# Token mixing with one level of Strassen: seven block products in place of eight, in two passes over the contraction tokens

## The chip, the cores and the metric

The kernel runs on one core of a Trainium2 chip. The metric is the device time of one execution in microseconds (us). Where there are several executions, the median is given with the lowest and highest. In the profile PE is TensorE (matrix multiplication), PEld its weight load, DVE is VectorE, ACT is ScalarE, POOL is GpSimd and SP is SyncE, which here only issues transfers; a "q" after an engine's name marks the engine's queue. "L384" is line 384 of the kernel that was profiled, so line numbers differ between variants.

## The reference

A long convolution per channel gives `y` (8 batches, 5696 tokens, 128 channels). Then comes the block that this study is about:

```python
theta = y @ w_theta                      # 128 x 128
zr, zi = y * cos(theta), y * sin(theta)  # "phases"
yr = einsum('ts,bsd->btd', w_tok_r, zr)  # token mixing: two 5696 x 5696 matrices
yi = einsum('ts,bsd->btd', w_tok_i, zi)
u = y + yr + yi
out = u + maximum(u @ w_ch, 0)           # w_ch 128 x 128
```

Token mixing is one product `[w_tok_r w_tok_i] x [zr; zi]`: 5696 output tokens, 2 x 5696 contraction tokens, 8 x 128 = 1024 columns. It is by far the largest part of the work.

## The kernel before

The kernel works in stages: convolution; phases of all 45 token tiles (128 tokens each), whose zr and zi go to memory; a load of all z tiles into SBUF; then token mixing, one output tile after the other. The core of the last stage, with cuts:

```python
z_sb = zp.tile([P, NK, BD], BF16)                 # all of zr and zi, NK = 89 contraction tiles
for c in range(NBC): ...                          # a few large loads on SyncE's queue

def load(ti, c, ng):                              # weights: 32-partition loads on GpSimd's queue
    wb = wp.tile([P, 4, BJ * 64 + REM], BF16, tag="wb")
    for i in range(4):
        nc.gpsimd.dma_start(wb[32 * i:32 * i + 32, :ng, :w], ...)
    return wb
# weights(): VectorE transposes 32 x 32 blocks of wb into wt            [cut]
# tail(): adds y, transposes, multiplies by w_ch, stores                [cut]
pend = []
for ti in range(NT):
    ps = [kps.tile([P, 512], F32, tag=f"ps{h}") for h in range(2)]   # pool kps has bufs=2
    for c in range(NBC):
        wb = load(ti, c, m // 32)
        for j0 in range(0, BJ, CJ):
            for k, wt in weights(wb, c, j0, min(CJ, BJ - j0), m // 32):
                for h in range(2):
                    nc.tensor.matmul(ps[h][:m], wt, z_sb[:, k, h * 512:(h + 1) * 512],
                                     start=(k == 0), stop=(k == NK - 1))
            if c < 2 and j0 == CJ and pend:
                tail(*pend.pop(0))                # the tile before is finished here
    pend += [(ti, m, ps[0], 0), (ti, m, ps[1], 1)]
```

Both accumulators are double-buffered, so that the next tile starts while the last one is evicted. And the finishing work of a tile stands in the middle of the next tile, where its inputs are long there.

## Time and profile before

The time is 2781.31 us, median of 2 runs (2780.08 to 2782.54).

The page of the profiled run gives busy times and, in 40 equal slices of the span, the busy tenths of each engine. "PEclk" is the granted clock of TensorE in tenths, "DMA" the busy tenths of the 16 transfer engines.

```profile
PE 2399.3 (86%) x15345; PEld 1314.6 (47%) x15345; DVE 1038.9 (37%) x1401; ACT 483.6 (17%) x401; POOL 494.1 (18%) x775
...
PE   4788888886332259999999999999999999999998
...
DVE  5544444445999012322232222322232223222231
...
PEclk7699999998555579999999999999999999999999
DMA  9977777776523985555555555555555555555552
```

Read across: the convolution fills the first nine slices. Then VectorE is at 9 while TensorE is at 3 (phases), then the transfers are at 9 and nearly nothing else works (the z loads), and from about slice 15 TensorE is full to the end.

The view by windows gives the same for stretches: start and end in us, length, busy time and instruction count of each engine, granted clock, transfer share and GB/s.

```profile
664.00:900.00 236.00, 83.92 (x720) 71.64 (x720) 229.37 (x225) 152.01 (x137) 102.66 (x45) 0.51 0.40 148
905.00:1035.00 130.00, 44.98 (x163) 17.92 (x164) 8.79 (x14) 0.00 (x0) 9.54 (x18) 0.63 0.99 211
1200.00:1600.00 400.00, 400.00 (x1979) 185.03 (x1978) 116.89 (x195) 12.59 (x20) 86.32 (x161) 1.00 0.56 95
```

| stage before | time | what limits it |
|---|---|---|
| convolution | to 664 us | not touched by the change |
| phases | 664 to 900 us | VectorE, 229 of 236 us busy: 5.2 us per tile |
| z loads | 900 to about 1028 us (the last lands at 1027.6) | transfers, share 0.99 at 211 GB/s |
| mixing | to the end | TensorE, 400 of 400 us busy at clock 1.00; 39.3 us per output tile |

In mixing a 512-column matrix product starts every 0.216 us (1300.00, 1300.22, 1300.43, ... in the timeline). The Trainium skill, "TensorE: Matmul & The Clock Gate", part 1, gives 215.7 ns for that size at full clock and 426.7 ns in the throttled state; the first agrees here. A full engine at full clock can only be relieved by fewer products.

### The profile page before, as it was taken

The page shows a single profiled execution, that of the slowest core. Times are in us where ns is not written, and L with a number is a line of the kernel's source. Part 1 is how long each engine was busy: PE and PEld are TensorE (multiplying, and loading weights), DVE is VectorE, ACT ScalarE, POOL GpSimd, SP SyncE. Part 2 cuts the span into 40 slices and gives each one's busy share as a digit, 9 for nine tenths or more (in the row PEclk, how much of TensorE's full clock was granted, in tenths as well). Part 3 has the DMA queues.
Part 4 walks back from the last instruction along what each step waited for, and adds up shares of the span by engine and source line. Part 5 has one row for each costly group of instructions (what it writes and reads, how often), then busy time and mean ns, then how long its engine had stood idle before and what let it go on. Part 6 is the DMA issues. An engine that isn't in the chain of part 4 may idle for free.

```text
span 2782.4 us, 36609 instructions
## 1 busy us (share of the span) xinstructions
PE 2399.3 (86%) x15345; PEld 1314.6 (47%) x15345; DVE 1038.9 (37%) x1401; ACT 483.6 (17%) x401; POOL 494.1 (18%) x775
## 2 busy tenths in 40 slices
PE   4788888886332259999999999999999999999998
PEld 1377777775332024444444444444444444444444
DVE  5544444445999012322232222322232223222231
ACT  3444344445665000000000000000000000000000
POOL 0000000001444002222222222222222222222220
PEclk7699999998555579999999999999999999999999
DMA  9977777776523985555555555555555555555552
GB/s 249 219 175 176 170 176 177 175 180 189 200 102 106 228 176 98 98 94 91 95 97 93 94 92 97 98 93 95 98 98 94 91 95 97 93 94 92 97 98 35
DMA packets 261108, 348.81 MB, mean 125 GB/s; under 512 B 27472, under 2 KB 221392, under 8 KB 260816
## 3 DMA queue, kind: packets, MB, share of 16 engines
q0 software_dynamic: 108384, 131.28, 30.8%
q1 hardware_dynamic: 152128, 213.56, 30.0%
q8 instruction: 121, 1.98, 0.3%
q10 hardware_dynamic: 432, 1.64, 0.2%
q14 instruction: 43, 0.35, 0.0%
HBM read 417.40 MB, written 60.23 MB: 172 GB/s over the span
## 4 chain that ended last, share of the span: by engine, by line
PE 72%; DMA 14%; DVE 9%; SPq 3%; issue 2%; ACT 0%; DVEq 0%; POOL 0%; ACTq 0%; POOLq 0%
PE psum L155 9%; DMA strip<-h_pad 9%; SPq L225 3%; DVE zr L194 2%; DVE mag L185 2%; DMA tmp<-in_x_dram 2%; DVE red L182 2%; DMA z_sb<-zi_hbm 2%; DVE yT L174 1%; DMA h_bf<-in_h_dram 1%; DVE strip L150 1%; DVE strip L144 1%; PE v L284 1%; PE utp L279 1%; PE ps_20849 L301 1%
## 5 line engine op out<-in xcount | busy, mean ns | idle before, releaser
L301 PEld LDWEIGHTS <-wt 128*128 128x128 bf16 (+1 forms) x7920 | 771.4, 98 | 997.1 <-issue 112.4
L255 DVE STREAM_TRANSPOSE wt<-wb 128x512 f32<-128x512 f32 (+1 forms) x540 | 357.0, 661 | 1219.8 <-PE ps_9186 L301 96.1
L155 PE MATMUL psum<-x_sb,strip 128*128 128x360 bf16 (+44 forms) x5760 | 483.2, 243 | 72.8 <-DVE strip L144 37.1
L155 PEld LDWEIGHTS <-strip 128*128 128x128 bf16 x5760 | 410.8, 98 | 146.0 <-DVE strip L144 42.9
L245 POOL DMA_DIRECT2D wb<-in_moe_w_tok_r_dram x360 | 194.6, 545 | 1445.2 <-DVE wt L255 1104.8
L276 ACT ACTIVATE ub<-u 128x512 bf16<-128x512 f32 (+1 forms) x90 | 56.7, 630 | 1821.4 <-DVE u L274 1821.4
L159 ACT ACTIVATE y_sb<-psum 128x360 bf16<-128x360 f32 x128 | 227.5, 1778 | 329.1 <-PE psum L155 329.1
L195 POOL TENSOR_TENSOR zi<-sin_sb,y_sb 128x1024 bf16<-128x1024 f32 x45 | 102.7, 2282 | 792.7 <-ACT sin_sb L189 784.5
L245 POOL DMA_DIRECT2D wb<-in_moe_w_tok_i_dram x360 | 194.6, 545 | 9.8 <-issue 9.5
L144 DVE COPY strip<-strip 64x2944 bf16<-64x2944 bf16 (+1 forms) x128 | 115.3, 904 | 164.2 <-DMA strip<-h_pad 150.2
L150 DVE COPY strip<-strip 64x2944 bf16<-64x2944 bf16 (+1 forms) x128 | 115.6, 906 | 159.6 <-DMA strip<-h_pad 131.3
L177 PE MATMUL theta_ps<-w_theta_sb,yT 128*128 128x128 bf16 x360 | 49.1, 308 | 144.1 <-DVE yT L174 144.0
L301 PE MATMUL ps_9185<-z_sb,wt 128*128 128x512 bf16 x88 | 39.2, 445 | 97.6 <-DMA z_sb<-zi_hbm 97.6
L177 PEld LDWEIGHTS <-yT 128*128 128x128 bf16 x360 | 35.2, 138 | 156.1 <-DVE yT L174 156.1
L113 PE MATMUL rps<-tmpbf,R_bf 128*128 128x512 bf16 x90 | 46.5, 620 | 50.5 <-DVE tmpbf L110 50.1
L194 DVE TENSOR_TENSOR zr<-cos_sb,y_sb 128x1024 bf16<-128x1024 f32 x45 | 84.2, 1874 | 4.3 <-ACT cos_sb L190 4.3
L286 DVE SCALAR_TENSOR_TENSOR u<-v,u 128x512 f32<-128x512 f32 (+1 forms) x90 | 62.2, 691 | 52.3 <-PE v L284 52.3
L185 DVE TENSOR_SCALAR mag<-red 128x1024 int32<-128x1024 int32 x45 | 69.6, 1580 | 0.0
L110 DVE CAST tmpbf<-tmp 128x1024 bf16<-128x1024 f32 x45 | 56.7, 1267 | 33.4 <-DMA tmp<-in_x_dram 33.2
L180 ACT ACTIVATE rnd<-theta_ps,magic 128x1024 f32<-128x1024 f32 x45 | 50.0, 1113 | 47.4 <-PE theta_ps L177 47.4
L115 ACT ACTIVATE x_sb<-rps 128x1024 bf16<-128x1024 f32 x45 | 46.1, 1024 | 58.2 <-PE rps L113 58.1
L190 ACT ACTIVATE cos_sb<-mag,half_pi 128x1024 f32<-128x1024 f32 x45 | 51.6, 1147 | 23.4 <-DVE mag L185 23.4
(306 smaller groups left out, 3504.0 us busy)
## 6 DMA issues: line engine op xcount, KB each, us to landing
strip<-h_pad SPq DMA_DIRECT2D x128, 376.0 KB, 4.4
wb<-in_moe_w_tok_r_dram POOLq DMA_DIRECT2D x264, 176.0 KB, 3.8
wb<-in_moe_w_tok_i_dram POOLq DMA_DIRECT2D x264, 176.0 KB, 4.9
strip<-h_pad SPq DMA_DIRECT2D x128, 360.0 KB, 5.1
tmp<-in_x_dram SPq DMA_DIRECT2D x44, 512.0 KB, 5.8
out_dram<-u SPq DMA_DIRECT2D x88, 256.0 KB, 2.3
wb<-in_moe_w_tok_r_dram POOLq DMA_DIRECT2D x88, 184.0 KB, 3.7
wb<-in_moe_w_tok_i_dram POOLq DMA_DIRECT2D x88, 184.0 KB, 5.7
```

Source lines behind the costliest of these rows:

```text
L144: nc.vector.tensor_copy(strip[64:, :w], strip[:64, 64:w + 64])
L150: nc.vector.tensor_copy(strip[:64, 64:w + 64], strip[64:, :w])
L155: nc.tensor.matmul(psum[:, B * k: B * k + B * ntj], strip[:, c:c + P], x_sb2[:, d, :B * ntj], start=(k == 0), stop=(k == NT - 1))
L159: nc.scalar.activation(y_sb[:, :, :, d].rearrange("q t b -> q (t b)"), psum, AF.Copy)
L177: nc.tensor.matmul(theta_ps[:, bb * D:(bb + 1) * D], yT[:, b, :], w_theta_sb, start=True, stop=True)
L185: nc.vector.tensor_scalar(mag.bitcast(mybir.dt.int32), red.bitcast(mybir.dt.int32), 0x7FFFFFFF, None, op0=ALU.bitwise_and)
L194: nc.vector.tensor_mul(zr, cos_sb, yflat)
L195: nc.gpsimd.tensor_mul(zi, sin_sb, yflat)
L225: nc.sync.dma_start(z_sb[32 * i:32 * i + 32, 2 * BJ * c:2 * BJ * (c + 1), :].rearrange("p (j r) n -> p j (r n)", r=2), bass.AP(tensor=zsrc ...
L245: nc.gpsimd.dma_start(wb[32 * i:32 * i + 32, :ng, :w], bass.AP(tensor=a.tensor, offset=a.offset + ti * P * S + (i % 2) * Q + c * BJ * 64, ...
L255: nc.vector.transpose(wt.rearrange("p j g t r -> p (j g t r)").bitcast(F32).rearrange("p (j g t) -> p g j t", j=CJ, g=4)[:, :ng, :nj], wb[ ...
L301: nc.tensor.matmul(ps[h][:m], wt, z_sb[:, k, h * 512:(h + 1) * 512], start=(k == 0), stop=(k == NK - 1))
```

## The change

Intent: split output tokens, contraction and columns in halves and form the 2 x 2 block product by Strassen's seven products M1 to M7 in place of eight. Two output tiles ("a pair": tile t and tile 22 + t) times 1024 columns are then made together, 7 accumulators of 128 x 512. The seven combinations of z are kept in SBUF for half of the tokens at a time (11 x 2 x 7 x 512 values of 2 bytes, 158 KB in each of 128 partitions), so the contraction is done in two passes of 22 tiles; pass 1 leaves partial results in memory and pass 2 adds them. Pass 1 needs the phases of only the first 22 tiles, and the other 23 are done as half tiles during pass 1. The 64 leftover tokens are done apart. The core of the diff, with cuts:

```diff
-    with tc.tile_pool(name="s2", bufs=3) as tsb, ...:         # phases of all 45 tiles
-        for ti in range(NT): ...
+        for ti in order:                                       # 22 tiles
+            phases(ti, y_sb[:, ti, :, :], 0, B, sb1, tps, thp)
...
+        def load_b(p):                                         # operand sums of one pass
+            for j in range(NJ):                                # NJ = 11
+                bt = bp.tile([P, 2, 7, 512], BF16, tag=f"b{j}")
+                tb = tbp.tile([P, 2, 2, 512], BF16, tag="tb")
+                for i in range(4):
+                    nc.sync.dma_start(bt[q, :, M2, :], z_rows(zr_hbm, r0, 2, 2, 0))
+                    nc.sync.dma_start(bt[q, :, M5, :], z_rows(zi_hbm, r0, 2, 2, 512))
+                    nc.sync.dma_start(tb[q, :, 0, :], z_rows(zr_hbm, r0, 2, 2, 512))
+                    nc.sync.dma_start(tb[q, :, 1, :], z_rows(zi_hbm, r0, 2, 2, 0))
+                nc.vector.tensor_sub(bt[:, :, M3, :], b12, b22)      # and four more
...
+        def finish(p, ti, h, c, m=P):
+            if p == 0:
+                nc.gpsimd.dma_start(c[:m], y2_hbm[ti]..., accum_op=add)   # c += y
+                nc.sync.dma_start(cp_hbm[ti]..., c[:m])                   # partial result
+                return
+            nc.gpsimd.dma_start(c[:m], cp_hbm[ti]..., accum_op=add)       # c += partial
+            # copy to bf16 (ACT), transpose (PE), copy (ACT), product with w_ch (PE), max and add, store
...
+        def pair(p, tt, bts, zl):
+            ms = [mps.tile([P, 512], F32, tag=f"m{q}") for q in range(7)]   # pool mps has bufs=1
+            for ci, (j0, nj) in enumerate(CHUNKS):                          # 3 chunks: 4, 4, 3 steps
+                a11 = w_t(moe_w_tok_r, top, p, j0, nj)   # 4 loads on GpSimd, 1 transpose on VectorE
+                a12 = w_t(moe_w_tok_i, top, p, j0, nj)
+                a22 = w_t(moe_w_tok_i, bot, p, j0, nj)
+                a21 = w_t(moe_w_tok_r, bot, p, j0, nj)
+                for q in (M5, M3, M4, M2, M1, M7, M6):
+                    if q == M5: a = w_sum(a11, a12, add, nj)                # VectorE
+                    elif q == M3: a = a11
+                    elif q == M4: a = a22
+                    elif q == M2: a = w_sum(a21, a22, add, nj)
+                    ...
+                    for j in range(nj):
+                        for r in range(2):
+                            nc.tensor.matmul(ms[q], a[:, j, :, r], bts[j0 + j][:, r, q, :], ...)
+                if p == 0:
+                    background(1 if ci < 2 else 0)       # a half tile of phases
+            nc.scalar.activation(c11, ms[M5], AF.Copy)
+            nc.vector.tensor_add(c12, ms[M3], c11)
+            nc.scalar.activation(c22, ms[M3], AF.Copy)
+            nc.vector.tensor_sub(c11, ms[M4], c11)
+            ...                                          # M2, M1, M7, M6 likewise
+            finish(p, tt, 1, c12); finish(p, 22 + tt, 0, c21)
+            finish(p, tt, 0, c11); finish(p, 22 + tt, 1, c22)
```

## The prediction

> **What bounds it now.** The stage windows show three parts: convolution to about 664 us; phases of 45 token tiles to 900 us (VectorE busy all the time, 5.2 us per tile); token mixing to the end. Mixing first waits for its z tiles (DMA busy share about 1.0 until about 1035 us). Then TensorE is 100% busy at granted clock 1.00: 1973 matmuls in 400 us, 39.3 us per output tile of 178 matmuls of 512 columns, so about 0.216 us each. That is the floor for this work; only fewer matmuls help. VectorE is 29% busy there, GpSimd (weight-load issues, 0.545 us each in the groups view) 22%.
>
> **What the change removes.** 8,010 wide matmuls become about 7,120: 22 pairs x 154 in each pass, plus leftovers. That is 890 x 0.216 = 190 us of TensorE. 23 of the 45 phase tiles leave the serial stage: 23 x 5.2 = 120 us. Loads before mixing halve: some 50 us. Gross gain 310 to 360 us.
>
> **What it adds, per pair (33.2 us of matmuls).**
> - VectorE: 12 transposes (0.71/0.58 us, 8 us), 15 bf16 sums (estimate 0.6 us for 1024 elements, two per cycle; the Trainium skill, "VectorE: DVE Perf Modes", "What auto-detection actually checks"; no run shows it yet), 8 PSUM additions at 0.65 us, and phases or final steps: about 26 us. Busy, not full.
> - GpSimd: 48 weight issues x 0.545 = 26 us, plus four accumulating loads: about 30 us.
> - Seven PSUM accumulators of one buffer each and one shared "misc" bank. Nothing is double-buffered across pairs, and VectorE, GpSimd and the DMA queue are in order.
>
> The instruction order shows what this costs. In a pair's last chunk VectorE evicts M3/M5 before it transposes a22 for M4, and evicts M4 before transposing a21 for M2: about 2 us of idle TensorE each. In pass 1 a half-tile of phases (transpose, copy, matmul, ACT, VectorE) sits in TensorE's order just there: 4 to 5 us more. At the pair's end GpSimd's accumulating loads wait for the last eviction, and the next pair's a22 and a21 loads stand behind them (landing 3.8 to 4.9 us in the DMA issues list). In pass 2 the final transposes and channel matmuls, which need the accumulated tile, stand in TensorE's order ahead of M4, through the single misc bank: another 7 us.
> I estimate 10 to 13 us of idle TensorE per pair, so 46 us in pass 1 and 48 in pass 2 (before: 2 x 39.3 = 78.7 per two output tiles; after: 94).
>
> **Sum.** Conv 664 + phases 115 + pair 0 with loading 80 + 21 x 46 + left rows 25 + pair 0 again 80 + 21 x 48 + end 35 = about 2970; I take 2940, as stalls may overlap. With only 6 us of stalls per pair it would be about 2740.
>
> Predicted 2940 us, 80% range 2760 to 3110. Faster by over 2%: 0.13; within 2%: 0.18; slower: 0.69.
>
> **What shows it.** Right: in steady pairs TensorE busy about 75 to 80%, its idle time ended by VectorE (transposes, sums) in the last chunk and first chunk; in pass 2 by ACT's copies for the final steps; pair period 44 to 50 us; a second load gap of 30 us or more between passes; granted clock dipping below 1. VectorE below 70%. The phase stage must end near 780 us.
> Wrong: pair period near 36 to 38 us with TensorE over 90% busy.
>
> **What would make it wrong.** Accumulating loads landing in 2 us and weight prefetch deep enough to hide the boundary (faster); sums at one element per cycle, slow 512-byte weight packets, or idle gaps halving TensorE's clock (slower).

## The result, and the profile after

The kernel takes 3258.15 us, median of 2 runs (3245.34 and 3270.97), and is correct. The ratio to the kernel before is 1.171, with a 95% interval of 1.152 to 1.191. It is 17% slower. The direction of the prediction was right, but the time lies 148 us above the upper end of its range.

The page of the changed kernel, the same lines as before:

```profile
PE 2415.1 (74%) x14377; PEld 1237.3 (38%) x14377; DVE 1612.0 (50%) x2462; ACT 623.1 (19%) x696; POOL 1536.0 (47%) x2598
...
PE   4788888942587777777777787578887787877777
...
DVE  5544444486465454544454545455554445454443
...
PEclk7899999955698888888888888789999999999898
DMA  9877777766576767676767667767768677776865
```

968 fewer PE instructions (the prediction had counted on 890) take 16 us more of PE time, because they no longer all run at full clock; and PE is never at 9 in mixing. No other engine is full either: this is a kernel of waits, not of work.

The windows: phases and the first loads (the last phase product ends at 772.9), the load ramp of pass 1, nine pairs of pass 1, and a stretch of pass 2.

```profile
664.00:780.00 116.00, 34.15 (x288) 29.14 (x288) 99.00 (x100) 66.08 (x62) 60.06 (x34) 0.50 0.53 186
798.00:870.00 72.00, 38.21 (x96) 12.23 (x97) 29.70 (x52) 0.00 (x0) 31.01 (x59) 0.67 0.62 118
1044.00:1528.00 484.00, 362.61 (x1526) 149.11 (x1526) 235.78 (x387) 51.31 (x81) 284.46 (x483) 0.87 0.68 108
2650.00:3150.00 500.00, 389.04 (x1863) 175.03 (x1862) 245.61 (x421) 61.76 (x105) 325.32 (x582) 0.93 0.73 97
```

A regular mark in the trace, ScalarE's last copy of an accumulator in each pair, gives the periods. They make the sum of the prediction measurable term by term:

| term | predicted | measured | excess |
|---|---|---|---|
| convolution and phases | 779 | 773 | -6 |
| first pair of pass 1, with loading | 80 | 133 | 53 |
| 21 pairs of pass 1 | 21 x 46 = 966 | 1097 (52.3 each; 53.5 in the steady part) | 131 |
| boundary: leftover rows, loading, first pair of pass 2 | 25 + 80 = 105 | 146 | 41 |
| 21 pairs of pass 2 | 21 x 48 = 1008 | 1045 (49.8 each; 51.5 in the steady part) | 37 |
| end | 35 | 49 | 14 |
| sum | 2973 | 3243 (span of the profiled run) | 270 |

Per steady pair of pass 1, the window gives 362.6 / 484 x 53.5 = 40.1 us of busy TensorE and 13.4 us idle. At 0.216 us the 154 products are 33.2 us, with the phases' small products about 34.2; so the half clock costs about 6 us. The idle time is what I had predicted (10 to 13 us); the clock was not in my sum. In pass 2 the idle time is 111.0 / 500 x 51.5 = 11.4 us, and the busy time again 40.1 us.

The waits of TensorE at the end of a pass-1 pair, from the timeline of PE (start, duration, operation, count; in brackets the idle time before and what ended it). In this view, every group of two products should last 0.59:

```profile
1520.94 0.61 PE L384 MATMUL m_12667<-b_8370,out__12940 128*128 128x512 bf16 x2 [0.73 <-DVE out__12940 L295]
...
1524.95 0.61 PE L384 MATMUL m_12666<-b_8370,wt 128*128 128x512 bf16 x2 [2.55 <-DVE wt L273]
...
1527.56 0.40 PE L174 MATMUL tpz<-ident_bf,yb 128*128 128x128 bf16 x4 [1.14 <-DMA yb<-y_hbm]
1528.47 0.40 PE L178 MATMUL theta_ps<-w_theta_sb,yT 128*128 128x128 bf16 x4 [0.52 <-DVE yT L175]
1531.97 1.03 PE L384 MATMUL m_12664<-b_8370,out__12960 128*128 128x512 bf16 x2 [3.10 <-DVE out__12960 L295]
1532.80 1.06 PE L384 MATMUL m_12664<-b_8393,out__12960 128*128 128x512 bf16 x2
...
1548.81 1.03 PE L384 MATMUL m_13018<-b_8186,wt 128*128 128x512 bf16 x2 [4.52 <-DVE wt L273]
```

After the waits the groups last 1.06 in place of 0.59, and start 0.85 us apart in place of 0.43: half clock (0.427 us per product, as the skill's page has it), until about 1537.9. The last wait, 4.52 us, belongs already to the next pair: its product M4, which needs a22 (loads from w_tok_i). VectorE's own timeline shows what stood before that transpose (the view names a load from w_tok_r; the a22 loads share their semaphores with others, and in the trace the last of them lands at 1547.96, just before the transpose), and GpSimd's queue shows why the weights came late (L303 is an accumulating load, L267 a weight load):

```profile
1548.05 0.71 DVE L273 STREAM_TRANSPOSE wt<-wb 128x512 f32<-128x512 f32 x1 [5.71 <-DMA wb<-in_moe_w_tok_r_dram]
```

```profile
1536.34 0.92 POOL L303 DMA_DIRECT2D c_12994<-y_hbm  x1 [4.88 <-DVE c_12994 L401]
1536.91 0.92 POOL L267 DMA_DIRECT2D wb<-in_moe_w_tok_i_dram  x1
1540.00 0.86 POOL L303 DMA_DIRECT2D c_12992<-y_hbm  x1 [2.17 <-DVE c_12992 L404]
1540.57 0.85 POOL L267 DMA_DIRECT2D wb<-in_moe_w_tok_i_dram  x1
1541.29 1.02 POOL L303 DMA_DIRECT2D c_12995<-y_hbm  x1
1541.86 1.57 POOL L267 DMA_DIRECT2D wb<-in_moe_w_tok_i_dram  x2
1542.95 2.65 POOL L267 DMA_DIRECT2D wb<-in_moe_w_tok_r_dram  x4
```

GpSimd issues in order. Its accumulating loads need the finished tile c, hence the last eviction, hence the end of the pair's last products; the next pair's four a22 loads stand between and behind them. The first is issued at 1536.91, the last two in the row that starts at 1541.86; the last lands at 1547.96, is transposed at 1548.05, and TensorE goes on at 1548.81. So the wait has two parts, the late issue and the landing, which took 5.6 us for the last load; over the whole run the median for loads of this size is 3.7 to 4.0 us. In pass 2 the wait before such a load is longer still, and the waits of TensorE are of three kinds (eviction ahead of a transpose, eviction ahead of a sum, finishing work that waits for ScalarE):

```profile
2687.05 0.92 POOL L307 DMA_DIRECT2D c_21112<-cp_hbm  x1 [11.57 <-DVE c_21112 L404]
```

```profile
2728.36 0.61 PE L384 MATMUL m_21204<-b_16567,wt 128*128 128x512 bf16 x2 [1.90 <-DVE wt L273]
...
2731.69 0.61 PE L384 MATMUL m_21202<-b_16567,out__21444 128*128 128x512 bf16 x2 [1.86 <-DVE out__21444 L295]
...
2745.19 0.40 PE L313 MATMUL utp<-ident_bf,ub 128*128 128x128 bf16 x4 [2.47 <-ACT ub L310]
```

ScalarE's copy in turn waited for the landing of the accumulating load, and so did the next one (TensorE waited 1.88 us for that):

```profile
2744.50 0.63 ACT L310 ACTIVATE ub<-c_21493 128x512 bf16<-128x512 f32 x1 [13.31 <-DMA c_21493<-cp_hbm]
...
2748.13 0.63 ACT L310 ACTIVATE ub<-c_21494 128x512 bf16<-128x512 f32 x1 [1.86 <-DMA c_21494<-cp_hbm]
```

In pass 2 these loads therefore hold TensorE through the finishing work; whether the weights behind them hold it there too is not shown.

The load ramp at the start of each pass, in SyncE's queue, VectorE beside it. Each of the 11 steps has 16 such issues, 0.64 us apart, on one queue:

```profile
805.26 0.59 SPq L251 DMA_DIRECT2D b_8232<-zi_hbm  x1
805.90 0.59 SPq L252 DMA_DIRECT2D tb<-zr_hbm  x1
806.53 0.59 SPq L253 DMA_DIRECT2D tb<-zi_hbm  x1
```

```profile
799.56 0.69 DVE L259 TENSOR_TENSOR b_8209<-b_8209 128x1024 bf16<-128x1024 bf16 x1 [6.16 <-DMA b_8209<-zi_hbm]
...
810.47 0.69 DVE L259 TENSOR_TENSOR b_8232<-b_8232 128x1024 bf16<-128x1024 bf16 x1 [7.73 <-DMA b_8232<-zi_hbm]
```

A step takes 10.7 us in the median (10.9 here, 799.56 to 810.47), and 16 x 0.64 = 10.2 us of it are the issues; some steps are longer, up to 13.4 us. SyncE's queue also waits until the sums have freed the single tile tb, about 10 us in the whole first ramp by the view of its waits. Meanwhile the transfers are not full: share 0.62, 118 GB/s, against 0.99 and 211 GB/s in the load stage of before.

So there are three theories for the 270 us of excess, not exclusive: the ramp is bound by issue on one queue (94 us in two terms); the pair is held by a chain through GpSimd's ordered queue (accumulating loads ahead of weight loads) and by the order of evictions on VectorE; or the half clock itself is the cost. Rivals: the engines or the transfers are at their limit with the new work.

### The profile page after: what moved, and what is told of

The parts are those of the page before. It is cut to its first block, busy times and chain, and to the rows that moved or that the text cites. A ratio compares the mean times of both kernels' runs of the same rounds, so it can differ in the third digit from the quotient of the medians.

```text
span 3243.6 us, 39671 instructions
## 1 busy us (share of the span) xinstructions
PE 2415.1 (74%) x14377; PEld 1237.3 (38%) x14377; DVE 1612.0 (50%) x2462; ACT 623.1 (19%) x696; POOL 1536.0 (47%) x2598
## 5 line engine op out<-in xcount | busy, mean ns | idle before, releaser
L267 POOL DMA_DIRECT2D wb<-in_moe_w_tok_r_dram x1080 | 636.4, 709 | 173.0 <-DVE wt L273 114.5
L267 POOL DMA_DIRECT2D wb<-in_moe_w_tok_i_dram x1080 | 638.9, 666 | 70.7 <-issue 17.6
L192 POOL TENSOR_TENSOR zi<-red,y_sb 128x1024 bf16<-128x1024 f32 x22 | 55.2, 2528 | 712.1 <-DMA y_hbm<-y_sb 663.5
L384 PEld LDWEIGHTS <-wt 128*128 128x128 bf16 x1936 | 197.7, 107 | 450.8 <-DVE wt L273 213.8
L181 ACT ACTIVATE red<-theta_ps,magic 128x512 f32<-128x512 f32 (+1 forms) x68 | 55.9, 823 | 865.8 <-PE theta_ps L178 853.4
L192 POOL TENSOR_TENSOR zi<-red,yb 128x512 bf16<-128x512 f32 x46 | 62.8, 1364 | 263.8 <-issue 219.3
L182 DVE SCALAR_TENSOR_TENSOR red<-red,theta_ps 128x512 f32<-128x512 f32 (+1 forms) x68 | 57.6, 857 | 154.3 <-ACT red L181 154.2
L313 PE MATMUL utp<-ident_bf,ub 128*128 128x128 bf16 (+1 forms) x360 | 44.0, 259 | 104.5 <-ACT ub L310 87.0
L315 ACT ACTIVATE uts<-utp 128x512 bf16<-128x512 bf16 (+1 forms) x90 | 53.3, 592 | 127.7 <-PE utp L313 127.7
L187 ACT ACTIVATE red<-red,zero_b 128x512 f32<-128x512 f32 (+1 forms) x68 | 58.3, 857 | 91.0 <-DVE mag L185 91.0
```

The lines of the kernel that those rows point to most:

```text
L182: nc.vector.scalar_tensor_tensor(red, red, MAGIC, theta_ps, op0=ALU.subtract, op1=ALU.subtract)
L187: nc.scalar.activation(red, red, AF.Sin, bias=zero_b, scale=-TWO_PI)
L192: nc.gpsimd.tensor_mul(zi, red, yflat)
L267: nc.gpsimd.dma_start(wb[32 * i:32 * i + 32, :ng, :nj * 64], bass.AP(tensor=a.tensor, offset=a.offset + row0 * S + p * H + i * QR + j0 * 6 ...
L313: nc.tensor.transpose(utp[:, b, :m], ub[:m, b, :], ident_bf[:m, :m])
L384: nc.tensor.matmul(ms[q], a[:, j, :, r], bts[j0 + j][:, r, q, :], start=(j0 + j == 0 and r == 0), stop=end and (zl is None or q not in (M6 ...
```

## The experiments

e1 to e7 are single runs beside a single run or several of the kernel before on the same chip; their state is unknown, and the changed kernel's own two runs differ by 26 us, so for them I read the periods rather than the last ten microseconds of the total. e8 to e10 are repeated. In e7 to e10 the partial result is stored in bf16 rather than f32.

### e1_ramp: the operand loads as one transfer over 128 partitions

```diff
-                           ap=[[step * BD, 32], [BD, n_in], [1, 512]])
+                           ap=[[QR * BD, 4], [step * BD, 32], [BD, n_in], [1, 512]])
...
-                for i in range(4):
-                    nc.sync.dma_start(bt[q, :, M2, :], z_rows(zr_hbm, r0, 2, 2, 0))       # 16 in a step
+                nc.sync.dma_start(bt[:, :, M2, :], z_rows(zr_hbm, r0, 2, 2, 0))           # 4 in a step
```

> Only the loading of the B factors is changed: one DMA over 128 partitions where there were four over 32 (4 issues per token step instead of 16), and the two extra operands land in the slots of M6 and M7, so the single shared staging tile is gone. Theory (the sync queue's issue time, 16 x 0.63 us = 10.3 us of the measured 10.7 us per step, bounds the first pair of each pass): a step falls to 4 to 6 us, the first pair of each pass from 110 to 135 us to 60 to 75 us, the kernel to 3130 to 3170 us. Rival (the transfers themselves bound it, 1 MB a step): steps stay at 10 us or more, time unchanged within 1%.

Measured: correct, 3379.54 us (before 2782.51): slower than the changed kernel by 121 us. The steps became 11.8 to 14.4 us, the boundary 196 us. The transfers of the ramp, in 40 slices of 0.8 us from 798 us on:

```profile
DMA  9697853332222222222222222899233322222222
GB/s 130 99 159 115 116 95 66 65 66 79 97 97 92 88 91 88 91 88 88 90 88 91 88 90 90 154 172 168 82 61 65 66 80 94 96 93 91 88 90 90
```

The share is stuck at 2 to 3 tenths and 88 GB/s: a quarter of the engines. The Trainium skill, "DMA: Bandwidth & Descriptors", "Rules for kernel authors", says that the outermost dimension of the pattern limits the number of engines used by a transfer; mine has an outermost dimension of 4, and the 256 KB loads follow one another at 2.9 us. The expectation (4 to 6 us per step) was missed. The edit traded one limit for another, so this run does not test the theory; it only shows that the number of issues is not the only way to lose the ramp.

### e2_noaccum: without the accumulating loads (wrong result)

```diff
-                nc.gpsimd.dma_start(c[:m], y2_hbm[ti]..., accum_op=add)
                 nc.sync.dma_start(cp_hbm[ti]..., c[:m])
...
-            nc.gpsimd.dma_start(c[:m], cp_hbm[ti]..., accum_op=add)
```

> Wrong result on purpose: the accumulating loads are left out in both passes; everything else stays. Theory (GpSimd's in-order queue holds the next pair's a22 and a21 loads behind accumulating loads that wait for the last eviction): the 4.5 us idle gap of TensorE ahead of M4 in the first chunk of pass 1 goes, the pair period there falls from 53.5 to 46 to 49 us, in pass 2 from 51 to 44 to 47 us, the kernel to 2950 to 3050 us. Rival (weight loads are limited by issue rate or by 512-byte packets, whatever stands between them): periods stay within 2 us of 53.5 and 51.

Measured: 2965.62 us, 293 us less than the changed kernel. Pass 1 has 48.3 us per pair (53.5), pass 2 42.7 (51.5), and in pass 2 the clock is at 1.00:

```profile
1044.00:1528.00 484.00, 378.25 (x1678) 162.03 (x1711) 270.14 (x434) 57.17 (x90) 281.64 (x502) 0.91 0.67 100
2400.00:2900.00 500.00, 433.25 (x2178) 194.29 (x2220) 293.90 (x505) 76.37 (x132) 347.67 (x650) 1.00 0.76 95
```

The wait of 4.5 us ahead of M4 is gone from the timeline. Pass 1 came out as expected, pass 2 below the expected 44 to 47. In pass 1 idle and busy TensorE fall together: per pair 10.5 us idle (from 13.4) and 37.7 us busy (from 40.1), as the clock rises with the waits gone. What is left in pass 2 is mainly two waits of 1.90 (at times 2.12) and 1.86 us, behind the two evictions. This is the largest effect of a single edit. The run takes away the transfers as well as their place in the queue; e7 keeps the data (as bf16) and changes the way, but two other things with it.

### e3_allphases: all 45 tiles' phases before mixing

```diff
+        order += list(range(22, NT))
...
-        bg = [(t, h) for t in range(22, NT) for h in range(2)]
+        bg = []
```

> All 45 tiles go through their phases before mixing, none during pass 1. Theory (the chain of transposes, VectorE and ScalarE work of two half tiles sits in TensorE's order and costs 8 to 10 us a pair): phase stage longer by 120 us, pass 1 pair period 53.5 to 43 to 46 us, the kernel 60 to 110 us faster, 3150 to 3200 us. Rival (the phases hide in idle time that other waits make anyway): period stays above 50 us and the kernel is 50 to 120 us slower than 3258.

Measured: correct, 3225.0 us. A pair of pass 1 takes 46.3 us, 7.2 less; the stage before is 126 us longer (mark of the first pair at 1032 against 906). Over the 21 periods 145 us are saved for 126 us spent. Period (43 to 46) and time (3150 to 3200) just miss the expectation; the rival, a period above 50, fails. So phases inside the pairs cost 7 us per pair in this order, more than they cost in their own stage (5.2 us per tile): moving them gained nothing that is clear of the 26 us between the changed kernel's own runs. This is a cost of placement, as e9 shows.

### e4_warm: keeping TensorE's clock up

```diff
+            KEEP = {(2, M4): 8, (2, M2): 5, (0, M4): 14}
...
+                    for w in range(pad):          # products with a zero weight, in the known waits of pass 1
+                        tc.keep_in_program_order(
+                            nc.tensor.matmul(ms[q], zw, bts[j0][:, 0, q, :], start=..., stop=False))
```

> 27 multiplications by a zero weight tile per pair of pass 1, put into TensorE's three long waits (ahead of M4 and M2 in the last chunk, ahead of M4 in the first); result unchanged. They add 5.8 us of work at full clock, and nothing else changes. Theory (5 to 6 us of a pass 1 pair is matmuls at half clock after idle gaps of 3 to 4.5 us): granted clock in pass 1 rises from 0.87 to 0.95 or more, period 53.5 to 48 to 51 us, the kernel 50 to 120 us faster; pass 2 unchanged. Rival (TensorE is not what the pair waits for, the loads and VectorE are): clock rises, period unchanged within 1 us or longer.

Measured: correct, 3234.1 us. The clock in pass 1 rises to 0.95 (from 0.87), but the period falls only to 52.6 us (from 53.5):

```profile
1095.00:1525.00 430.00, 356.02 (x1580) 153.40 (x1611) 213.98 (x353) 46.67 (x72) 260.87 (x442) 0.95 0.70 111
```

The expected period, 48 to 51, was missed. Without the fillers' 5.8 us TensorE is busy 356.0 / 430 x 52.6 - 5.8 = 37.7 us per pair (from 40.1): 2.4 of the 6 us of half clock are gone, and 0.9 us of that reach the period (1.6 as the mean of all 21 periods; the two runs of the changed kernel differ by 0.6 us per pair). The rest comes back as waits, when the next data are not there yet. The test is partial: the compiled order put the fillers only in part where the waits are (2.83 us ahead of M2's products stay empty, at 1459.77), and what full clock alone would bring stays open.

### e5_ramp2: the operand loads on two queues

```diff
-                tb = tbp.tile([P, 2, 2, 512], BF16, tag="tb")
...
-                    nc.sync.dma_start(bt[q, :, M5, :], z_rows(zi_hbm, r0, 2, 2, 512))
-                    nc.sync.dma_start(tb[q, :, 0, :], z_rows(zr_hbm, r0, 2, 2, 512))
-                    nc.sync.dma_start(tb[q, :, 1, :], z_rows(zi_hbm, r0, 2, 2, 0))
+                    nc.scalar.dma_start(bt[q, :, M5, :], z_rows(zi_hbm, r0, 2, 2, 512))
+                    nc.sync.dma_start(bt[q, :, M6, :], z_rows(zr_hbm, r0, 2, 2, 512))
+                    nc.scalar.dma_start(bt[q, :, M7, :], z_rows(zi_hbm, r0, 2, 2, 0))
```

> The operand loads of a pass keep their 32-partition form, but half of them are issued from ScalarE's queue and half from SyncE's, straight into the final tile. If the 16 issues of 0.59 to 0.64 us each on the one queue set the 10.7 us step of the ramp (my theory), the step falls to 5.3 to 6 us, the first pair of pass 1 and the boundary between the passes each get about 50 us shorter (135 to about 85, 145 to about 95), the periods of the other pairs stay at 53.5 and 51.5, and the kernel takes 3130 to 3190. Rival: the transfers or VectorE's operand sums set the step; then it stays at 9 us or more and the kernel within 2% of 3258.

Measured: correct, 3209.59 us. The first pair is done 28.7 us sooner (877.7 against 906.4) although the phases happened to end 11 us later (784.0 against 772.9), so the ramp is 40 us shorter; its ten steps take 73.6 us in place of 113.1. The boundary is 31.2 us shorter (114.3 against 145.5), and the other periods stay within 0.6 us on average. A step takes about 7.4 us. The ramp's window:

```profile
798.00:870.00 72.00, 47.08 (x136) 13.47 (x135) 45.67 (x77) 0.90 (x2) 40.26 (x77) 0.78 1.00 193
```

The share went from 0.62 to 1.00 and the rate from 118 to 193 GB/s. The issue on one queue was the limit, as the theory says, but only 31 to 40 of the expected 50 us per pass come back, the step stays above the expected 5.3 to 6 us and the time above 3130 to 3190. The likely reason is that the transfers are the next limit, near the 211 GB/s of the kernel before. They are not the operands alone: from 800 to 840 us GpSimd's queue takes half of the transfer engines' time (52.5%) for 2.37 of 7.98 MB. And the edit also drops the tile tb, for which SyncE had waited about 10 us in the first ramp, so part of the gain may come from that.

### e6_late: two evictions behind the last sum

```diff
-            nc.vector.tensor_add(c12, ms[M3], c11)
+            with tc.issue_after(last_sum[0].ins):      # VectorE's order only, no wait
+                nc.vector.tensor_add(c12, ms[M3], c11)
...
-            nc.vector.tensor_sub(c11, ms[M4], c11)
+            with tc.issue_after(last_sum[0].ins):
+                nc.vector.tensor_sub(c11, ms[M4], c11)
```

> VectorE's evictions of M3 and M4, which wait for the end of their products, are queued behind the last operand sum of the same pair. If they hold up the transposes and sums of the last chunk (my theory for the two idle gaps of 1.9 us per pass-2 pair and those of 2.5 and 3.1 us in pass 1), those gaps vanish: pass 2 falls from 51.5 to 47.5 to 48.5 per pair, pass 1 from 53.5 to 50 to 51.5, the kernel to 3090 to 3170. Rival: these gaps are made by the weight loads or by VectorE's own throughput; then the gaps only move and the periods stay within 1 us.

Measured: correct, 3238.98 us. Pass 2 falls to 47.8 us as expected, and its two waits of 1.9 us are gone. Pass 1, expected at 50 to 51.5, rises from 53.5 to 55.9, and the time misses the expected 3090 to 3170. GpSimd's queue shows why:

```profile
1509.45 0.92 POOL L305 DMA_DIRECT2D c<-y_hbm  x1 [4.53 <-DVE c L399]
```

L399 is the delayed eviction. The accumulating load of c12 now waits 4.53 us for it, and the next pair's weights wait behind that load. One mend alone moved the wait from VectorE's queue to GpSimd's.

### e7_three: three mends together, with a correct result

The loads of e5, the order of e6, and in place of the accumulating load:

```diff
-            nc.gpsimd.dma_start(c[:m], cp_hbm[ti]..., accum_op=add)
+            nc.vector.tensor_add(c[:m], c[:m], ci[:m])       # ci: fetched by SyncE in the pair's first chunk
```

> Correct. Three mends together: the operand loads on two queues, VectorE's evictions of M3 and M4 behind the last sum, and no accumulating load on POOL's queue (the old partial, now bf16, is fetched by SyncE early in the pair, and VectorE adds it: 4 more VectorE operations of about 0.6 us per pair). If the excess over my sum is made of the load ramp, of POOL's weight loads queued behind the accumulating loads, and of the early evictions, the periods fall to 45 to 48 in pass 1 and 39 to 42 in pass 2 and the kernel takes 2740 to 2860; without the ordering in one queue the late evictions no longer cost pass 1 anything. Rival: VectorE, which then has about 35 us of work per pair, becomes the limit and pass 2 stays above 44; or the waits only move, and the kernel stays above 2900.

Measured: correct, 2818.31 us (before 2786.38, median of 7 runs). Pass 1 has 44.4 us per pair, pass 2 41.1. Both lie in the expected stretch or below it, and no cost of the late evictions is left to be seen in pass 1 (no run takes them alone out of this version). 440 us of the changed kernel's 3258 went with these three mends, with the same products and the same work on VectorE plus four additions per pair. Two things beside order and issue changed with them: the accumulating transfers are plain loads now, and the partial result has half the bytes.

### e8_deferred: the finishing steps of pass 2 spread over the next pair

```diff
             ub = cp.tile([P, 4, D], BF16, tag="yb")
             nc.scalar.activation(ub..., c..., AF.Copy)
+            yield                                    # one stage after each product of the next pair
             utp = mps.tile([P, 4, P], BF16, tag="misc", name="utp")
...
                     if ci < 2:
+                        advance()
```

> Correct. As the three mends, and in pass 2 the transposes and channel products that finish a pair are spread between the products of the next pair's first two chunks, one stage per product, so that TensorE never waits for ScalarE's copies between them (0.5 to 2.5 us, four to six times a pair, in the trace of the changed kernel). If those gaps are additive, pass 2 falls by another 2 to 4 us per pair to 36 to 39, pass 1 stays as in the three mends, and the kernel takes 2680 to 2790. Rival: VectorE's queue fills the room, and pass 2 does not fall below 40.

Measured: correct, 2818.7 us, median of 4 runs, ratio to before 1.012 (95% interval 1.010 to 1.014). Pass 2 stays at 41.1 us. The expectation was missed: the waits (2.13 us for ScalarE's copy, 0.75 us behind it) are the same ones as in e7, whose compiled order had spread the finishing steps after the first already. The source's order was not what TensorE executed, so the edit changed little.

### e9_pipelined: the order pinned by hand

The order of TensorE, VectorE and ScalarE in mixing is written out and pinned; the phases' product on GpSimd goes to VectorE, and the copy of their transposed tile to ScalarE. The core, with cuts:

```diff
+                prod(M1, k.s1)                       # last chunk of a pair; k2 is the next pair's first chunk
+                nc.vector.tensor_sub(c22, c22, ms[M2])
+                nc.vector.tensor_add(c21, ms[M2], c21)
+                s5(k2)                               # VectorE: first sum of the next pair
+                advance()                            # one stage of phases or of finishing
+                prod(M7, k.s7)
+                tr_bot(k2)                           # VectorE: transposes of the next pair
+                nc.vector.tensor_add(c11, ms[M1], c11)
+                nc.vector.tensor_add(c22, ms[M1], c22)
...
+        for ins in traced[pinned_from:]:             # TensorE, VectorE, ScalarE: order as written
+            tc.add_manual_dep(ins, prev[ins.engine].name, ...)
```

> Correct. The deferred variant with the order on TensorE, VectorE and ScalarE pinned by hand: VectorE transposes and sums the next chunk's weights one to three products ahead, each eviction follows the product that ends its bank and sits between the next pair's weight operations, the product on POOL (zi) moves to VectorE and the copy of the transposed tile to ScalarE, phases and finishing steps advance one stage per product. If what is left of the excess are fixed waits between queues (2.5 and 3.6 us per pass-1 pair, 2.1 and 0.8 us in pass 2, and the half clock after them), pass 1 falls from 44.4 to 38 to 41, pass 2 from 41.1 to 37 to 39, and the kernel takes 2620 to 2720, 3 to 6% under the kernel before. Rival: the engines or the transfers are at their limit; then it stays at 2780 or more.

Measured: correct, 2699.24 us, median of 4 runs (2694.16 to 2705.09), ratio to before 0.968 (0.966 to 0.970). Pass 1 falls to 34.4 us per pair, further than the expected 38 to 41; pass 2 rises to 43.2 where 37 to 39 were expected. That the total is inside the expected 2620 to 2720 is luck: the two misses cancel. Pass 1's window:

```profile
1000.00:1450.00 450.00, 449.27 (x2227) 207.96 (x2226) 361.05 (x618) 88.92 (x144) 336.96 (x627) 1.00 0.97 138
```

TensorE is busy 449 of 450 us at clock 1.00, with the phases still inside. That settles the rival for pass 1 (with zi moved from GpSimd to VectorE): neither VectorE (80% busy) nor GpSimd (75%) was a limit, nor were the transfers, though their share of 0.97 says that they are near one now. The 7 us of phases were placement: 154 products at 0.216 us are 33.2 us, so about 1 us is left for them. Nobody tended the clock here; it came back when the waits went. In pass 2 I had made a wait of my own. The product over the leftover tokens needs the one "misc" bank, whose eviction I had put behind the next pair's transposes:

```profile
2312.67 0.59 PE L549 MATMUL left<-zl,wlt 128*128 128x512 bf16 x1 [5.80 <-DVE c L539]
```

### e10_leftover: the leftover products in the banks of M3, M4, M6, M7

The core of the change against e9, with cuts (the comment sums up the edit):

```diff
-                left12 = mps.tile([P, 512], F32, tag="misc", name="left")
-                nc.tensor.matmul(left12, wlt, zl[:, 512:], start=True, stop=True)
+                # last chunk: M3 += wlt*zl2, M4 += wlb*zl1, M7 += (wlt-wlb)*zl1, M6 += (wlb-wlt)*zl2
+                nc.tensor.matmul(ms[q], wz[q], zl[:, 512 * (q in (M3, M6)):][:, :512], start=False, stop=False)
```

> Correct. The pipelined kernel, whose pass 1 runs at 34.4 us per pair with TensorE without a wait but whose pass 2 takes 43.2, with one 5.8 us wait per pair at the product over the 64 leftover tokens (it has one bank, and its eviction stands behind the next pair's weight transposes on VectorE). Here the leftover products go straight into the banks of M3, M4, M6 and M7, in the last chunk, with the difference of the two leftover weights for M7 and M6; no bank and no eviction of their own. If that wait and the half clock after it are the whole difference to pass 1 beside about 2 us of finishing work on TensorE, pass 2 falls to 36 to 38.5 and the kernel to 2540 to 2610. Rival: VectorE or the transfers hold pass 2; then it stays above 40.

Measured: correct, 2608.8 us, median of 4 runs (2606.57 to 2610.17); before in the same rounds 2785.94 us, median of 7; ratio 0.937 (0.935 to 0.939). Pass 1 stays at 34.4 us, pass 2 falls to 38.8:

```profile
1000.00:1450.00 450.00, 449.29 (x2230) 207.94 (x2228) 360.11 (x616) 89.73 (x145) 337.04 (x627) 1.00 0.96 138
2200.00:2600.00 400.00, 361.47 (x1892) 170.78 (x1890) 252.65 (x455) 69.12 (x116) 277.64 (x517) 0.98 0.79 107
```

Pass 2 misses the expected 36 to 38.5 by 0.3 us, but not by the rival's measure (above 40); the total is just inside the expected range. In the timeline one wait of 1.9 us for ScalarE's copy is left in each pair, and some for VectorE's sums. What is left of the load ramps (the first pair is done 118 us after the phases, the boundary takes 121 us; in e7 it was 98 and 108) was not tried further. This version is 6.3% faster than the kernel before and 20% faster than the changed kernel as given.

## Why the prediction was right or wrong

- **The floor before, right.** TensorE was full at full clock, and 39.3 us per tile could only fall by fewer products. e10 shows what the seven products are worth: 34.4 us per pair in pass 1, where two tiles for half the contraction would have been 39.3 before.
- **Work removed, right.** The phase stage ended at 773 us, predicted 779, and 968 products were saved, predicted 890.
- **Work added, right.** Sums of 1024 bf16 elements took 0.69 us in a single record and start about 0.60 us apart (800.24, 800.85, 801.45 in VectorE's timeline), against the estimate of 0.6 from the skill's page "VectorE: DVE Perf Modes", "What auto-detection actually checks": the trace agrees. VectorE stayed at 50%, as predicted "busy, not full".
- **Where TensorE would wait, right in kind.** "VectorE evicts M3/M5 before it transposes a22 for M4, and evicts M4 before transposing a21 for M2: about 2 us of idle TensorE each" was measured as 1.90 and 1.86 us in pass 2. The phases at the wrong place, the accumulating loads ahead of the weights and the finishing work that waits for the accumulated tile are all in the trace. In pass 1 the idle time was 13.4 us, the upper edge of "10 to 13 us".
- **The step that failed: "so 46 us in pass 1 and 48 in pass 2".** This added the idle time to 33.2 us of products at full clock. Measured were 53.5 and 51.5 us in the steady parts (52.3 and 49.8 on average): 131 and 37 us too little in the sum. The idle time was about as predicted; the mis-sized term is the busy time, 40.1 us in both passes. In pass 1 about 1 us of the difference is the phases' small products and about 6 us are products that ran at 0.427 us each after the long waits. The prediction named a lower clock among its signs and its risks, and left it out of its sum; it even took 30 us off the sum "as stalls may overlap". How much a full clock alone would bring is open: e4 took away 2.4 of these 6 us and the period fell by 0.9. What brought both down is taking the waits away: without the accumulating loads (e2) pass 1 lost 5.2 us per pair, 2.9 of idle and 2.4 of busy time, and pass 2 lost 8.8; with the order pinned and all else that e9 changed, pass 1 lost 19.1 and the clock was at 1.00. The waits come from the chain last product, eviction, accumulating load, weight load, transpose, next product, through two in-order queues, and in pass 2, as far as the trace shows, from the finishing work that waits for the accumulating loads to land.
- **The second term that failed: "pair 0 with loading 80", twice.** Measured were 133, and 146 for the boundary with its leftover rows (predicted 105): 94 us together. I had counted bytes ("loads before mixing halve: some 50 us") and not issues. 16 issues of 0.64 us on one queue make 10.2 of the step's 10.7 us; with two queues and without the tile tb (e5) 40 and 31 us came back, then the share of the transfers was 1.00.
- **A term nearly right.** "48 weight issues x 0.545 = 26 us": in the changed kernel one record lasts 0.67 to 0.71 us on average, but these records overlap (two of them start 0.57 us apart and last 0.92 in the lines above). GpSimd's busy time for the 2160 issues is 1275 us, 0.59 each, so 28 us per pair. With the accumulating loads alone taken out (e2) a record lasts 0.55 us and the busy time per issue is 0.54: the accumulating loads do slow the issues beside them, by some 2.5 us per pair.
- **The falsifier was sound.** "Pair period near 36 to 38 us with TensorE over 90% busy" is what the last version does (34.4 and 38.8): the change was good, its schedule was not.

Still open: how the 5.2 to 8.8 us of e2 split between the transfers themselves and their place in the queue. e7 changed the way and the type of the data, the eviction order and the ramp at the same time.

## What to carry to other kernels

When a change removes work from a full engine, the gain comes only if that engine stays full: list for each in-order queue what stands ahead of the instruction that feeds it at each boundary, and add the waits along the chain, with the issues counted as well as the bytes. Put nothing that waits for the end of one block of work (an accumulating load, an eviction, a finishing step) ahead of the loads or transposes of the next block in the same queue. Mend such waits together and pin the order: one alone (e6) may only move the wait, and the order in the source (e8) need not be the order that runs.

## What the Trainium skill lacked or had wrong

- "DMA: Bandwidth & Descriptors", "Issuing engines are not separate DMA queues", says that issuing from several engines saves only the sequencer's time, "which is usually small relative to the DMA itself". With 64 KB loads it was the limit here: 16 issues of 0.64 us made 10.2 us of a 10.7 us step, and a second issuing queue raised the transfer share from 0.62 to 1.00 and the rate from 118 to 193 GB/s. The page could add a check: issue interval times number of loads, against bytes over rate.
- The same page says that an accumulating load must be issued from GpSimd ("Rules for kernel authors"), but draws no consequence for the other loads that GpSimd issues: here such a load waited 11.57 us for an eviction (8 to 16 us over the pairs of pass 2), with the next block's weight loads behind it, and taking those loads out was worth 293 us of 3258.
- "TensorE: Matmul & The Clock Gate", part 1: both rates agree (0.216 and 0.427 us for 512 columns). The page could say that filling the waits with products need not shorten the whole: raising the clock from 0.87 to 0.95 with fillers bought 0.9 us of 53.5 (not clear of the runs' differences), while removing the waits brought it to 1.00 by itself.
- Nothing wrong was found in the rule "Use all 16 engines" of "DMA: Bandwidth & Descriptors": in e1 an outermost dimension of 4 gave 88 GB/s and 2.9 us for 256 KB.
